# Attention and a gated feed-forward on one core: score matmuls whose weights are widened from 112 to 128 columns

## The chip, the core and the metric

The kernel runs on one core of one Trainium2 chip. The metric is the time of one execution in microseconds on the device. Before the change, the median of six runs is 487.43 us (486.87 to 487.92).

A core has engines that work side by side and meet through semaphores: TensorE (PE) for matmuls, with its weight loads listed on their own (PEld), VectorE (DVE), ScalarE (ACT), GpSimd (POOL) and SyncE (SP). In this kernel POOL issues the loads from memory, and SP issues the transposing DMAs and the stores of the output.

## What is computed

Eight batches of twelve heads, 448 positions of 64 values each. Attention with a squared relu instead of a softmax, then a feed-forward layer with a SiLU gate:

```python
scores = scale * np.matmul(q, k.transpose(0, 1, 3, 2))
attn = np.maximum(scores, 0.0) ** 2 / S
x = np.matmul(attn, v)            # then (batch, seq, heads * dim) = 3584 x 768
xn = x / rms * rms_g
g = xn @ w_gate                   # 768 -> 1536
out = (g * sigmoid(g) * (xn @ w_val)) @ w_out
```

Inputs and output are float32; the kernel's matmuls take bfloat16.

## The kernel before

**Layout.** The two heads of a pair `j` (six pairs) lie one above the other on partitions 0 to 63 and 64 to 127. For each batch a tile `qkT` of shape [128, 6, 2, 448] holds the transposed Q (index 0 of the third axis) and the transposed K (index 1). A position of the sequence is `4 p + c`; the 448 keys are taken as four chunks `c` of 112.

**Scores** (`scores`, line 193) are called for two chunks at a time, so twelve times per batch. For each chunk, two matmuls, one per head, take 112 columns of K as weights and the 448 columns of Q as the moving operand, each with 64 rows: the two heads use the two halves of the array's rows. The profile writes the shape of such weights as 64*112. The results of a chunk fill a PSUM tile `psS` of two banks; two such tiles exist. ScalarE, or VectorE for some last chunks, applies the relu (`r`, lines 211 and 213), and VectorE squares it (line 216).

**The rest of attention.** `attend` (line 224) multiplies the squares with V: weights of 112 rows and 64 columns, two heads side by side on the two halves of the columns. `norm` (line 270) sums squares with a matrix of ones and scales; its result `xn` feeds the feed-forward.

**Feed-forward** (`ffn`, line 340). `gate` and `value` run six matmuls each for each of twelve blocks of 128 columns (`psG`, `psV`, line 295, weights 128*128). `outproj` (line 318) runs twelve matmuls per half tile (`psO`, line 321), ScalarE copies the result, SP stores it.

**Order.** The program's order on each engine is written out by hand. `merge` (line 18) weaves the attention and the norm of batch `b + 1` between the feed-forward units of batch `b`, up to 85% of them. A score call thus stands between gate and value units, or before an `attend`.

**Transposes of Q and K.** Batches 0 and 1 are transposed on TensorE: `transposes` (line 166) writes eight transposes of Q and eight of K for a head pair into one PSUM tile `psT`, and VectorE copies that tile to `qkT`. Batch 1's first step stands at the head of the feed-forward of batch 0. For batches 2 to 7, `transpose_dma` (line 103) issues eight transposing DMAs on SP, four for Q and four for K, after two thirds of the feed-forward of batch `b - 2`. POOL's loads of batch `b + 2` are issued as the feed-forward of batch `b` begins, in the order Q, K, V, into two buffers each.

**Start.** POOL loads Q, K and V of batch 0 in pieces, then the gate and value weights, Q, K and V of batch 1 and the output weights. `keep_busy` puts idle matmuls between the pieces of batch 0.

Of the kernel before, what the change touches and what calls it, by code (L numbers as in the profile page):

```python
# [8 lines left out]
FP32 = mybir.dt.float32  # L9
# [3 lines left out]
ACT = mybir.ActivationFunctionType  # L13
# [23 lines left out]
def kernel(  # L37
# [11 lines left out]
    nc = tc.nc  # L49
    P = nc.NUM_PARTITIONS  # L50
    B, H, S, D = q.shape
# [3 lines left out]
    PC = S // NCH  # L55
# [18 lines left out]
    ps_s = ctx.enter_context(tc.tile_pool(name="ps_s", bufs=2, space=bass.MemoryType.PSUM))  # L74
# [6 lines left out]
    qkT = {}  # L81
# [18 lines left out]
    def new_qkT(b):  # L100
        qkT[b] = qtpool.tile([P, HP, 2, S], BF16, name="qkT", tag="qkT")

    def transpose_dma(b):
        new_qkT(b)
        for ti, nm in enumerate(("q", "k")):
            for c in range(NCH):
                nc.sync.dma_start_transpose(
                    out=qkT[b][:, :, ti, c * PC : (c + 1) * PC], in_=ld[nm, b][:, c, :]
                )
# [56 lines left out]
    def transposes(b, j):  # L166
        if j == 0:
            new_qkT(b)
        psT = ps_m.tile([P, 2, S], BF16, name="psT", tag="mm")
        for ti, nm in enumerate(("q", "k")):  # L170
            for c in range(NCH):
                for hh in range(2):
                    nc.tensor.transpose(  # L173
                        out=psT[hh * D : (hh + 1) * D, ti, c * PC : (c + 1) * PC],
                        in_=ld[nm, b][:, 2 * j + hh, c * D : (c + 1) * D],
                        identity=ident[:],
                    )
        nc.vector.tensor_copy(out=qkT[b][:, j, :, :], in_=psT[:])
# [4 lines left out]
    def relu_on(b, j, c):  # L183
        return "dve" if c == 3 and (b or j % 2) else "act"

    def square_on(b, j, c):
        return "dve"

    def flush():
        while pending:  # L190
            pending.pop(0)()

    def scores(b, j, cs):
        pss = []
        for c in cs:
            psS = ps_s.tile([PC, 2, 512], FP32, name="psS", tag="psS")
            for hh in range(2):
                prt = slice(hh * D, (hh + 1) * D)
                nc.tensor.matmul(  # L199
                    out=psS[:, hh, :S],  # L200
                    lhsT=qkT[b][prt, j, 1, c * PC : (c + 1) * PC],
                    rhs=qkT[b][prt, j, 0, :],
                    start=True,
                    stop=True,
                )
            pss.append(psS)
        squares = []
        for c, psS in zip(cs, pss):
            r = apool.tile([PC, 2, S], BF16, name="r", tag="r")
            if relu_on(b, j, c) == "dve":  # L210
                nc.vector.tensor_relu(out=r[:], in_=psS[:, :, :S])  # L211
            else:
                nc.scalar.activation(out=r[:], in_=psS[:, :, :S], func=ACT.Relu)  # L213
            eng = nc.gpsimd if square_on(b, j, c) == "pool" else nc.vector
            squares.append(
                lambda r=r, eng=eng: eng.tensor_tensor(out=r[:], in0=r[:], in1=r[:], op=ALU.mult)  # L216
            )
            rsq[b, j, c] = r
        flush()
        pending.extend(squares)  # L220
# [25 lines left out]
    def attention(b):  # L246
        units = []

        def add(cost, *fns):
            units.append((cost, lambda: [f() for f in fns]))  # L250

        if b < PE_T:
            add(0.4, lambda: transposes(b, 0))
        for j in range(HP):
            add(0.5, lambda j=j: scores(b, j, (0, 1)))
            if b < PE_T and j + 1 < HP:
                add(0.4, lambda j=j: transposes(b, j + 1))
            if b == 0:
                add(0.3, lambda: keep_busy(2))
            add(1.2, lambda j=j: scores(b, j, (2, 3)), lambda j=j: j and attend(b, j - 1))  # L260
            if b == 0:
                add(0.3, lambda: keep_busy(2))
        add(0.1, flush)
        add(0.8, lambda: attend(b, HP - 1), flush)
        return units
# [88 lines left out]
    for b in range(B):  # L354
        side = []
        if b + 1 < B:
            side = attention(b + 1) + [(1.1, lambda b=b: norm(b + 1))]
        main = ffn(b)
        if b + 2 < B:
            for nm in ("q", "k", "v"):  # L360
                load(nm, b + 2)
            at = len(main) * 2 // 3
            main[at:at] = [(0, lambda b=b: transpose_dma(b + 2))]
        for fn in merge(main, side, 0.0, 0.15):
            fn()
# [30 lines left out]
```

## Time and profile before

| | |
|---|---|
| Median of six runs | 487.43 us |
| The profiled execution, its time | 487.58 us |
| Its span, first to last instruction | 485.8 us |
| Mean granted TensorE clock | 0.986 |
| PE busy | 460.9 us, 95% |
| DVE, ACT, POOL busy | 284.2, 253.6, 50.7 us |
| Score matmuls on the chain that ended last | 9% |

The busy time of an engine is the sum of its instructions' time without overlap. Matmuls are pipelined, so that a busy PE is not PE at its peak. The chain that ended last follows the work back from the last instruction, at each step to what released it or to the instruction before it on its engine. Where a row has three durations, they are the shortest, the middle and the longest in nanoseconds; `x384` counts instructions. A timeline line gives the start and the length of a merged group in microseconds, and in brackets the idle time before it with what ended that. Only what lies within the asked stretch is merged into a line.

### The profile page before, as it was taken

What the parts mean: (1) busy time and instruction counts of PE and PEld (TensorE: products, weight loads), DVE (VectorE), ACT (ScalarE), POOL (GpSimd) and SP (SyncE); (2) the same over time, 40 slices, a digit from 0 to 9 for tenths busy, and PEclk for the clock granted to TensorE, in tenths of its full rate; (3) what the DMA queues carried; (4) which work ended last, traced back from release to release, by engine and by line L of the source; (5) the groups of instructions that cost most, each with busy time, mean ns of one, the idle gap of its engine ahead of it and who ended that gap; (6) DMA issues with size and microseconds to landing.
All of it is one profiled execution on the core that took longest, in us unless ns stands there. A gap on an engine that the chain in (4) does not pass through costs nothing.

```text
span 485.8 us, 7099 instructions
## 1 busy us (share of the span) xinstructions
PE 460.9 (95%) x2872; PEld 220.4 (45%) x2872; DVE 284.2 (59%) x452; ACT 253.6 (52%) x372; POOL 50.7 (10%) x45
## 2 busy tenths in 40 slices
PE   7970999999999999999999999999999999999995
PEld 3420444454445544454445544454445544455553
DVE  2875377756663576765663577765664577662310
ACT  4870355456654566547654566547554566533221
POOL 8323001140001200040001300000000000000000
PEclk9996899999999999999999999999999999999999
DMA  9999999999301990099501992067101300021013
GB/s 108 200 204 199 209 161 135 112 158 178 47 1 36 190 182 9 0 122 198 64 1 34 189 162 33 1 121 119 28 1 34 97 2 0 1 65 34 0 34 97
DMA packets 128032, 43.32 MB, mean 89 GB/s; under 512 B 100608, under 2 KB 124416, under 8 KB 128000
## 3 DMA queue, kind: packets, MB, share of 16 engines
q0 software_dynamic: 88944, 23.60, 50.6%
q1 hardware_dynamic: 39056, 19.28, 21.1%
q8 instruction: 22, 0.36, 0.3%
q14 instruction: 10, 0.08, 0.1%
HBM read 47.19 MB, written 11.01 MB: 120 GB/s over the span
## 4 chain that ended last, share of the span: by engine, by line
PE 87%; DMA 8%; POOL 1%; DVE 1%; ACT 1%; issue 0%; POOLq 0%
PE psG L295 24%; PE psV L295 23%; PE psO L321 22%; PE psS L199 9%; PE psAV L228 8%; DMA kb<-in_k_dram 5%; DMA wv_sb<-in_moe_w_val_dram 3%; PE psSS L273 1%; DVE xn L284 1%; PE psT L173 1%; DVE rstd L281 1%; POOL kb L93 0%; POOL qb L93 0%; ACT r L213 0%; POOL vb L93 0%
## 5 line engine op out<-in xcount | busy, mean ns | idle before, releaser
L213 ACT ACTIVATE r<-psS 112x896 bf16<-112x896 f32 x147 | 128.5, 915 | 47.9 <-PE psS L199 45.0
L295 PE MATMUL psG<-xn,wg_sb 128*128 128x448 bf16 x576 | 127.0, 356 | 0.9 <-DVE xn L284 0.9
L295 PE MATMUL psV<-xn,wv_sb 128*128 128x448 bf16 x576 | 125.7, 355 | 0.0
L312 DVE TENSOR_TENSOR hT<-sil,psV 128x448 bf16<-128x448 bf16 x96 | 59.6, 621 | 99.3 <-PE psV L295 78.3
L321 PE MATMUL psO<-wo_sb,hT 128*128 128x512 bf16 (+1 forms) x672 | 112.9, 326 | 0.0
L216 DVE TENSOR_TENSOR r<-r 112x896 bf16<-112x896 bf16 x192 | 110.0, 618 | 0.2 <-ACT r L213 0.2
L306 ACT ACTIVATE sil<-psG 128x448 bf16<-128x448 f32 x96 | 52.2, 544 | 87.2 <-PE psG L295 86.8
L321 PEld LDWEIGHTS <-hT 128*128 128x128 bf16 x672 | 64.8, 98 | 47.5 <-issue 3.9
L295 PEld LDWEIGHTS <-wv_sb 128*128 128x128 bf16 x576 | 54.2, 98 | 58.1 <-issue 11.2
L295 PEld LDWEIGHTS <-wg_sb 128*128 128x128 bf16 x576 | 51.9, 98 | 62.4 <-issue 18.9
L328 ACT COPY ost<-psO 128x512 f32<-128x512 f32 (+1 forms) x56 | 26.8, 479 | 81.2 <-PE psO L321 81.2
L199 PE MATMUL psS<-qkT 64*112 64x448 bf16 x384 | 57.5, 372 | 3.0 <-ACT r L213 2.3
L211 DVE TENSOR_SCALAR r<-psS 112x896 bf16<-112x896 f32 x45 | 48.9, 1088 | 17.6 <-PE psS L199 17.6
L228 PE MATMUL psAV<-r,vb 112*64 112x448 bf16 x384 | 46.1, 359 | 0.8 <-DVE r L216 0.8
L281 DVE RECIPROCAL rstd<-rstd 128x448 f32<-128x448 f32 x8 | 23.6, 2953 | 22.6 <-ACT rstd L278 22.6
L199 PEld LDWEIGHTS <-qkT 64*112 64x112 bf16 x384 | 18.2, 125 | 38.8 <-issue 35.9
L241 DVE TENSOR_TENSOR x<-xT 128x448 bf16<-128x448 bf16 x48 | 18.6, 386 | 25.1 <-ACT xT L239 25.1
L239 ACT ACTIVATE xT<-psAV 128x448 bf16<-128x448 f32 x48 | 26.1, 544 | 10.4 <-PE psAV L228 7.2
L93 POOL DMA_DIRECT2D vb<-in_v_dram x9 | 8.1, 901 | 212.0 <-PE psAV L228 157.5
L284 DVE SCALAR_TENSOR_TENSOR xn<-xT,g_sb,rstd 128x448 bf16<-128x448 bf16 x48 | 29.3, 680 | 0.3
L228 PEld LDWEIGHTS <-vb 112*64 112x64 bf16 x384 | 17.8, 109 | 24.6 <-issue 16.7
L95 POOL DMA_DIRECT2D qb<-in_q_dram x6 | 13.8, 2304 | 34.8 <-DMA qkT<-kb 32.0
(28 smaller groups left out, 111.2 us busy)
## 6 DMA issues: line engine op xcount, KB each, us to landing
qb<-in_q_dram POOLq DMA_DIRECT2D x7, 672.0 KB, 14.1
kb<-in_k_dram POOLq DMA_DIRECT2D x7, 672.0 KB, 22.5
vb<-in_v_dram POOLq DMA_DIRECT2D x7, 672.0 KB, 9.1
out_dram<-ost SPq DMA_DIRECT2D x8, 336.0 KB, 4.4
wg_sb<-in_moe_w_gate_dram POOLq DMA_DIRECT2D x4, 576.0 KB, 18.5
wv_sb<-in_moe_w_val_dram POOLq DMA_DIRECT2D x4, 576.0 KB, 20.2
wo_sb<-in_moe_w_out_dram POOLq DMA_DIRECT2D x2, 1152.0 KB, 28.7
out_dram<-ost SPq DMA_DIRECT2D x8, 288.0 KB, 4.7
```

Source lines behind the costliest of these rows:

```text
L199: nc.tensor.matmul(out=psS[:, hh, :S], lhsT=qkT[b][prt, j, 1, c * PC : (c + 1) * PC], rhs=qkT[b][prt, j, 0, :], start=True, stop=True,)
L211: nc.vector.tensor_relu(out=r[:], in_=psS[:, :, :S])
L213: nc.scalar.activation(out=r[:], in_=psS[:, :, :S], func=ACT.Relu)
L216: lambda r=r, eng=eng: eng.tensor_tensor(out=r[:], in0=r[:], in1=r[:], op=ALU.mult)
L228: nc.tensor.matmul(out=psAV[hh * D : (hh + 1) * D, :], lhsT=ld["v", b][:, 2 * j + hh, c * D : (c + 1) * D], rhs=rsq[b, j, c][:, hh, :], st ...
L281: nc.vector.reciprocal(out=rstd[:], in_=rstd[:])
L284: nc.vector.scalar_tensor_tensor(out=xn[:, kt, :], in0=xTs[b][:, kt, :], scalar=g_sb[:, kt : kt + 1], in1=rstd[:], op0=ALU.mult, op1=ALU.mult,
L295: nc.tensor.matmul(out=ps[:], lhsT=w_sb[:, kt, fb * P : (fb + 1) * P], rhs=xns[b][:, kt, :], start=(kt == 0), stop=(kt == KT - 1),)
L306: nc.scalar.activation(out=s[:], in_=psG[:], func=ACT.Silu)
L312: nc.vector.tensor_tensor(out=hTs[b // 2][:, fb, o : o + S], in0=sil[b, fb][:], in1=psV[:], op=ALU.mult)
L321: nc.tensor.matmul(out=ps[:, :w], lhsT=hTs[i][:, fk, t * P : (t + 1) * P], rhs=wo_sb[:, fk, o : o + w], start=(fk == 0), stop=(fk == FT - 1),)
L328: nc.scalar.copy(out=ost[:, o : o + w], in_=ps[:, :w])
```

## The change

K now comes first in `qkT` (index 0) and Q second (index 1), on both ways of transposing. The score matmul's weights begin at the chunk's first key, as before, and are 128 columns long: the chunk's 112 keys and the 16 columns that follow in the tile. For the chunks 0 to 2 these are keys of the next chunk, for chunk 3 the first 16 columns of Q. `psS` has 128 partitions, of which the relu reads the first 112. The number of instructions on each engine stays the same.

```diff
 def transpose_dma(b):
-        for ti, nm in enumerate(("q", "k")):
+        for ti, nm in enumerate(("k", "q")):
             for c in range(NCH):
                 nc.sync.dma_start_transpose(
...
 def transposes(b, j):
-        for ti, nm in enumerate(("q", "k")):
+        for ti, nm in enumerate(("k", "q")):
...
 def scores(b, j, cs):
-            psS = ps_s.tile([PC, 2, 512], FP32, name="psS", tag="psS")
+            psS = ps_s.tile([P, 2, 512], FP32, name="psS", tag="psS")
...
-                    lhsT=qkT[b][prt, j, 1, c * PC : (c + 1) * PC],
-                    rhs=qkT[b][prt, j, 0, :],
+                    lhsT=qkT[b][prt, j].rearrange("p t s -> p (t s)")[:, c * PC : c * PC + P],
+                    rhs=qkT[b][prt, j, 1, :],
...
-                nc.vector.tensor_relu(out=r[:], in_=psS[:, :, :S])
+                nc.vector.tensor_relu(out=r[:], in_=psS[:PC, :, :S])
...
-                nc.scalar.activation(out=r[:], in_=psS[:, :, :S], func=ACT.Relu)
+                nc.scalar.activation(out=r[:], in_=psS[:PC, :, :S], func=ACT.Relu)
```

## The prediction

> **What bounds the kernel now.** I read the busy rows of the page first, then the chain that ended last, then the instructions of the score line, and last the timeline of single score calls.
>
> ```profile
> PE 460.9 (95%) x2872; PEld 220.4 (45%) x2872; DVE 284.2 (59%) x452; ACT 253.6 (52%) x372; POOL 50.7 (10%) x45
> ...
> PE 87%; DMA 8%; POOL 1%; DVE 1%; ACT 1%; issue 0%; POOLq 0%
> PE psG L295 24%; PE psV L295 23%; PE psO L321 22%; PE psS L199 9%; PE psAV L228 8%; DMA kb<-in_k_dram 5%; DMA wv_sb<-in_moe_w_val_dram 3%; PE psSS L273 1%; DVE xn L284 1%; PE psT L173 1%; DVE rstd L281 1%; POOL kb L93 0%; POOL qb L93 0%; ACT r L213 0%; POOL vb L93 0%
> ```
>
> TensorE carries 87% of the chain and the score matmuls 9%, so a nanosecond taken from a score call is a nanosecond of the span, except where something else ended last. The 8% of DMA is one stretch at the start: the chain of waits in order of time shows K of batch 1 landing at 48.39 us, eight transposes of it, and then the first gate matmul; from there it is PE nearly without a break. Score calls before 48 us are therefore covered.
>
> What does a score call pay for its weights? The rows of the score line and of the attend line, and the timeline of one call, its successor, and an attend, answer that.
>
> ```profile
> L199 PEld LDWEIGHTS <-qkT x384: 122/123/127, 7.5 to 420.4; 64*112 64x112 bf16 x192
> L199 PE MATMUL psS<-qkT x384: 345/393/394, 7.5 to 420.6; 64*112 64x448 bf16 x192
> ```
>
> ```profile
> L228 PE MATMUL psAV<-r,vb x384: 349/353/378, 13.9 to 427.3; 112*64 112x448 bf16 x192
> ```
>
> ```profile
> 253.21 0.40 PE L199 MATMUL psS<-qkT 64*112 64x448 bf16 x2
> ...
> 253.44 0.35 PE L199 MATMUL psS<-qkT 64*112 64x448 bf16 x2
> 253.73 0.36 PE L295 MATMUL psG<-xn,wg_sb 128*128 128x448 bf16 x1
> ...
> 253.93 0.35 PE L295 MATMUL psG<-xn,wg_sb 128*128 128x448 bf16 x1
> ...
> 256.62 0.38 PE L228 MATMUL psAV<-r,vb 112*64 112x448 bf16 x2
> ...
> 256.83 0.36 PE L228 MATMUL psAV<-r,vb 112*64 112x448 bf16 x2
> ```
>
> A call is two pairs: the two heads run side by side on the two halves of the rows. [...] The open load is the difference between first and second start. Steady 448-column matmuls follow each other every 0.189 us (six psG take 1.31 us). After a change the second starts 0.20 us after the first for 128*128 weights, 0.21 for 64 columns of V, 0.23 for 112 columns of K; to the nanosecond 200, 213 and 233. The durations say the same: the first score pair takes 394 ns against 349 for the second (45 more), the first attend pair 378 against 353 (25 more), the first psG about 10 more. So 64 columns cost 25 ns, 112 columns 45 ns, 0.4 ns a column; full 128 columns cost only 10. The trace also records how a load reads its source: 112 columns as one run, the 128-column loads as four runs of 32. The changed program as built has the four-run form for all 384 score loads.
>
> **The change part by part.**
>
> *The load of 128 columns.* The second pair's load lies under the first pair's matmul in either form, so only one open load counts per call: 8 batches x 6 head pairs x 2 calls = 96 calls, less the 12 of batch 0, which lie before 48 us. Of the 84 left, two lose their gain: around 92 us the second pair of a call waits for ScalarE (the call at 91.55 has its second pair at 92.11, ended by the relu), and ScalarE's order there began with the silu at 89.90, so the call at 89.79 and the first pair at 91.55 give nothing. 82 count. No row shows a 64-row load of 128 columns. Its bounds: the 128*128 row, 10 ns, giving 233 - 200 = 33 ns saved; and 0.4 ns a column, 51 ns, giving 6 ns lost. I take 33, because the form of the load is that of the 128*128 row. 82 x 33 ns = 2.71 us gained.
>
> *Sixteen more columns to drain.* From the second pair to the next kind of matmul it takes 282 ns to psG; from 128*128 psV to a score call also 282, from 64-column psAV to psG 285. No order by columns: between -3 and +4 ns (a 128-column matmul lasts 353, the second score pair 349). I take +2: 82 x 2 = 0.17 us lost.
>
> *K before Q in the PE transposes of batches 0 and 1.* The 16 transposes of a step stand in order on PE, before everything after them. K lands last. Before, Q's eight ran while K was on its way:
>
> ```profile
> 44.96 0.59 PE L173 MATMUL psT<-ident,qb 112*64 112x112 bf16 x8 [10.06 <-DMA qb<-in_q_dram]
> 48.44 0.58 PE L173 MATMUL psT<-ident,kb 112*64 112x112 bf16 x8 [2.89 <-DMA kb<-in_k_dram]
> 48.95 0.93 PE L295 MATMUL psG<-xn,wg_sb 128*128 128x448 bf16 x2
> ```
>
> Now they come after K's. This is on the path: gate matmuls queue behind them. The granted clock there is 0.50 (38.98 to 52.6 us); four pairs of K's transposes start 92 to 97 ns apart, so Q's cost 4 x 93 = 0.37 us. If the clock rises at the same instant as before, the cold work pushed past it runs twice as fast, and 0.19 us is lost; if it rises that much later, 0.37. I take 0.37. The same happens at three waits for K in batch 0, at most 0.37 us each, 1.1 us; that is covered by the wait for K of batch 1: the last xn ends at 42.70 and the first gate matmul starts at 48.95. Without that cover it would be the 1.1 us.
>
> *K before Q in the DMA transposes of batches 2 to 7.* All eight issues of a batch move past each other in SP's queue. For batch 2, SP waited for Q's load until 68.06 and issued K's without waiting at 76.96, so K's landing is between; all eight now start between 68.1 and 77.0, take 14.7 us to issue and at most 10.6 to land: 102.3 at worst, and the first score call of batch 2 is at 107.23. On POOL, the load of Q of batch 3 waits for Q's transposes of batch 2, which now come last: 81.64 becomes at worst 102, its K load a little over 2 us later, V and the loads of batch 4 (98.58 to 101.48) behind them. Landing 22.5 us later and transposed in another 26, batch 3's K and Q stand at 153; its first score call is at 165.60, and SP's next output DMA at 152.28 waits for a late tile anyway. Later batches have their loads landed long before and 30 us between transposes and scores. Cost nothing; without cover it would be the whole delay, up to 20 us once.
>
> *A wider psS, the columns that are not read, the relu on 112 rows.* psS already takes two banks; ScalarE and VectorE read the same 112 rows. The neighbouring columns that a load now also reads (the next keys, or Q behind the last chunk) land with the same batch's transposes. Nothing.
>
> Sum: -2.71 + 0.17 + 0.37 = -2.17 us. The profiled execution took 487.58 us with a span of 485.8; it would become 485.4. It stands 0.15 above the median of the runs, 487.43, which would become 485.3.
>
> [...]
>
> **The rivals.**
>
> *The two halves load one after the other.* Each fast, 2 x 10 ns open: about 23 saved per call, 1.89 - 0.54 = 1.35 us, 486.1 us. For it: no row shows two fast loads at once. Against: the 112-column halves start 2 to 3 ns apart and overlap fully. Chance 0.07.
>
> *Half the rows load at the ordinary rate.* The place is the open first load: 51 ns instead of 45. It costs 82 x 6.4 = 0.53 us, plus 0.54 for drain and start: +1.07, 488.5 us, slower. It decides from the point where the open load takes over about 38 ns (45 less 0.54 us / 82). For it: every load under 128 rows or 128 columns in this trace follows 0.4 ns a column, and none of 64 rows is fast. Against: those loads also had fewer columns and one-run reads. Chance 0.12.
>
> *The clock rises one step later at the start.* From the first gate matmul at 48.95 to the rise at 52.63 the clock stays at 0.50 for 3.7 us. How the rise follows the work is not in the trace; if it came later by that length once more, half of it would be lost, at most 1.8 us, and I price it at 1.7: -2.17 + 1.7, 486.9 us, no change that counts. Against: PE is busy from the same landing of K on. Chance 0.05.
>
> **How the numbers follow.** The forecast has 0.76; its own range is 484.7 to 485.9 (saving 30 to 35 ns, drain -3 to +4 ns, start 0.19 to 0.37 us, and 0.3 us for runs that spread from 486.87 to 487.92). The 8-in-10 range reaches down to 484.5 and up to 486.9, over the serial halves and the late clock, and leaves out the ordinary rate. A measurement of this kernel can tell about 0.2%, 0.97 us, from no change: faster is below 486.46. Forecast and serial halves are faster (0.81 with a little off for the edge), the late clock is no change, and the ordinary rate lies at that edge, mostly slower.
>
> **What would show it.** Right: first score pairs near 360 ns instead of 394, pair starts about 200 ns apart, score loads below 123 ns, and an otherwise equal order of work. The first gate matmul 0.37 us later after K's landing. Wrong: first pairs at 400 ns or more (ordinary rate), near 375 (serial), waits of score loads for a DMA or for the copy of psT, or a clock of 0.50 past 55 us.

## The result: 485.26 us, and the profile after

The changed kernel takes 485.26 us (median of 21 runs) against 487.39 us (44 runs of the kernel before); the ratio is 0.9956, with a 95% interval of 0.9947 to 0.9964. The profiled execution took 486.15 us with a span of 484.4 us.

The page of the changed kernel, its busy row and its chain:

```profile
PE 457.5 (94%) x2872; PEld 213.9 (44%) x2872; DVE 284.1 (59%) x452; ACT 253.2 (52%) x372; POOL 50.7 (10%) x45
...
PE 86%; DMA 8%; POOL 1%; DVE 1%; ACT 1%; issue 0%; POOLq 0%
PE psG L296 24%; PE psV L296 23%; PE psO L322 22%; PE psS L200 8%; PE psAV L229 8%; DMA kb<-in_k_dram 5%; DMA wv_sb<-in_moe_w_val_dram 3%; PE psSS L274 1%; DVE xn L285 1%; PE psT L173 1%; DVE rstd L282 1%; POOL kb L93 0%; POOL qb L93 0%; ACT r L214 0%; POOL vb L93 0%
```

The instruction counts of the busy row are the same, and of the chain's lines only the score line gave something up (9% to 8%). PE is busy 3.4 us less, more than the time fell, since this sum also counts the twelve calls of batch 0, which lie under waits. Where in a call that happened is read from the score line's own rows (shortest, middle, longest duration):

```profile
L200 PEld LDWEIGHTS <-qkT x384: 91/93/97, 7.9 to 418.9; 64*128 64x128 bf16 x192
L200 PE MATMUL psS<-qkT x384: 345/359/361, 7.9 to 419.1; 64*128 64x448 bf16 x192
```

A load takes 93 ns instead of 123. The longest matmul, that of a first pair, which carries the open load, went from 394 ns to 361. The timeline shows one call: last psV, first pair, second pair, attend.

```profile
255.49 0.35 PE L296 MATMUL psV<-xn,wv_sb 128*128 128x448 bf16 x1
255.77 0.36 PE L200 MATMUL psS<-qkT 64*128 64x448 bf16 x2
...
255.97 0.35 PE L200 MATMUL psS<-qkT 64*128 64x448 bf16 x2
256.25 0.38 PE L229 MATMUL psAV<-r,vb 112*64 112x448 bf16 x2
```

The pairs start 0.20 us apart instead of 0.23. Over the 84 calls of batches 1 to 7 the middle values in the trace's nanoseconds are:

| ns, middle of 84 calls | before | after |
|---|---|---|
| previous matmul to first pair | 282 | 285 |
| first pair to second pair | 233 | 200 |
| second pair to the next kind | 284 | 284 |

So a call gives back 33 ns and takes 3. In the changed kernel each half's first matmul starts 4 ns after its own load; before, it was 1 to 2 ns. The two halves' loads start 3 ns apart in both kernels, so that now both precede the first matmul. The second pair's loads start 189 ns ahead of their matmuls (187 before), under the first pair's.

At the start, the transposes of batch 1 and the first gate matmuls of the changed kernel:

```profile
49.35 0.58 PE L173 MATMUL psT<-ident,kb 112*64 112x112 bf16 x8 [14.33 <-DMA kb<-in_k_dram]
49.72 0.58 PE L173 MATMUL psT<-ident,qb 112*64 112x112 bf16 x8
50.24 1.30 PE L296 MATMUL psG<-xn,wg_sb 128*128 128x448 bf16 x3
```

Q's eight transposes now stand between K's and the gate: 0.89 us from K's first transpose to the first gate matmul, against 0.51 before. K itself landed 0.9 us later in this execution; a second profile of the same kernel had it at 48.62, close to the 48.44 of the kernel before.

The queues of SP and POOL after the new order, from the timeline:

```profile
74.43 6.48 SPq L107 DMA_TRANSPOSE qkT<-kb  x4
80.96 5.26 SPq L107 DMA_TRANSPOSE qkT<-qb  x4
```

```profile
88.52 2.28 POOL L95 DMA_DIRECT2D qb<-in_q_dram  x1 [37.97 <-DMA qkT<-qb]
```

SP now waits for K's load and starts at 74.43 instead of 68.14; Q of batch 3 is loaded from 88.52 instead of 81.64. Neither is late: batch 2's first score call runs at 107.96 and waits for nothing there.

### The profile page after: what moved, and what is told of

Read it like the earlier page. It is cut to its first block, busy times and chain, and to the rows that moved or that the text cites. A ratio compares the mean times of both kernels' runs of the same rounds, so it can differ in the third digit from the quotient of the medians.

```text
span 484.4 us, 7098 instructions
## 1 busy us (share of the span) xinstructions
PE 457.5 (94%) x2872; PEld 213.9 (44%) x2872; DVE 284.1 (59%) x452; ACT 253.2 (52%) x372; POOL 50.7 (10%) x45
## 4 chain that ended last, share of the span: by engine, by line
PE 86%; DMA 8%; POOL 1%; DVE 1%; ACT 1%; issue 0%; POOLq 0%
PE psG L296 24%; PE psV L296 23%; PE psO L322 22%; PE psS L200 8%; PE psAV L229 8%; DMA kb<-in_k_dram 5%; DMA wv_sb<-in_moe_w_val_dram 3%; PE psSS L274 1%; DVE xn L285 1%; PE psT L173 1%; DVE rstd L282 1%; POOL kb L93 0%; POOL qb L93 0%; ACT r L214 0%; POOL vb L93 0%
## 5 line engine op out<-in xcount | busy, mean ns | idle before, releaser
L214 ACT ACTIVATE r<-psS 112x896 bf16<-112x896 f32 x147 | 128.3, 914 | 46.4 <-PE psS L200 46.1
L212 DVE TENSOR_SCALAR r<-psS 112x896 bf16<-112x896 f32 x45 | 48.9, 1088 | 16.7 <-PE psS L200 16.7
L200 PE MATMUL psS<-qkT 64*128 64x448 bf16 x384 | 54.2, 355 | 3.5 <-ACT r L214 2.8
L200 PEld LDWEIGHTS <-qkT 64*128 64x128 bf16 x384 | 11.7, 94 | 39.6 <-issue 37.7
L173 PE MATMUL psT<-ident,kb 112*64 112x112 bf16 x96 | 4.8, 226 | 15.3 <-DMA kb<-in_k_dram 15.3
```

Of the source, the lines that this page charges most:

```text
L200: nc.tensor.matmul(out=psS[:, hh, :S], lhsT=qkT[b][prt, j].rearrange("p t s -> p (t s)")[:, c * PC : c * PC + P], rhs=qkT[b][prt, j, 1, :] ...
L212: nc.vector.tensor_relu(out=r[:], in_=psS[:PC, :, :S])
L214: nc.scalar.activation(out=r[:], in_=psS[:PC, :, :S], func=ACT.Relu)
```

## Experiments

The theory: all of the gain is the open weight load of a score call, fast at 128 columns but not at 112 or 127, and the K-first order of the transposes costs 0.37 us at the start. The rivals: the gain comes of the order, of a wide psS, or of every load; and the fast load suffers from half rows or odd places.

Total times alone cannot part these by 0.1%, since runs of one kernel spread by 1 to 3.5 us. So I also took from each profile the stretch between the first gate matmuls of neighbouring batches, which holds twelve score calls and no part of the start. Three such stretches, and the time from the first pair to the second:

| kernel | pair to pair, ns | batch 2 to 3, us | 3 to 4 | 6 to 7 |
|---|---|---|---|---|
| before | 233 | 52.91 | 56.81 | 52.30 |
| after, two profiles | 200 | 52.54 | 56.44 | 51.96 |
| order only, 112 columns | 233 | 52.91 | 56.81 | 52.30 |
| Q transposed first, two profiles | 200 | 52.54 | 56.44 | 51.96 |
| 127 columns | 241 | 53.00 | 56.90 | 52.38 |
| 128 columns for one head | 200 and 234 | 52.91 | 56.81 | 52.30 |
| 128 columns in the first pair | 200 | 52.54 | 56.44 | 51.96 |
| 128 columns in the second pair | 233 | 52.91 | 56.81 | 52.30 |
| chunks of a call swapped | 200 | 52.54 | 56.44 | 51.96 |

The stretches repeat to 0.01 us between executions. The second distance of the kernel with one wide head is that of its narrow head, counted from the call's first matmul. 0.34 to 0.37 us for twelve calls is 28 to 31 ns a call, the 30 of the table before.

**Order only.** K first in tile and transposes, 112 columns.

```diff
-psS = ps_s.tile([P, 2, 512], ...)
+psS = ps_s.tile([PC, 2, 512], ...)
-lhsT=qkT[b][prt, j].rearrange("p t s -> p (t s)")[:, c * PC : c * PC + P],
+lhsT=qkT[b][prt, j, 0, c * PC : (c + 1) * PC],
```

> Both orders (tile and transposes) are K first, the weights stay 112 columns. Theory (the gain is the open weight load of a call): no gain is left, second pairs start 233 ns after first ones as before, and the start pays 0.37 us: 487.8 us, 0.1% over the kernel before, hardly to be told from it. The profile shows the first gate matmul about 0.89 us after K of batch 1 has landed, against 0.51 before. Rival (the gain comes of where K and Q stand, not of the load): 485.3 us.

Measured: 488.29 us against 487.85 on the same chip, ratio 1.0009 (0.9995 to 1.0024). Each stretch is that of the kernel before, and from K's first transpose to the gate it takes 0.89 us. The order gives nothing; the rival falls.

**Q transposed first**, K still first in the tile; run twice, the second time beside the changed kernel itself.

```diff
-for ti, nm in enumerate(("k", "q")):
+for ti, nm in ((1, "q"), (0, "k")):
```

> As the changed kernel, but Q is transposed first again on both ways; K still stands first in the tile. Theory: keeps the loads (pair starts 200 ns apart) and gets back the 0.37 us of Q's transposes at half clock after K has landed: 484.9 us, and the first gate matmul 0.51 us after K's landing. Rival (the lost time at the start is only a later landing of K, which has nothing to do with the order): 485.3 us.

> The changed kernel itself, on the same chip as the next three, so that they can be set beside it. 0.4% to 0.5% under the kernel before; between the first score call's two pairs 200 ns, first gate matmul 0.89 us after K's landing.

> Q transposed first again, beside the changed kernel on one chip. Theory: 0.37 us less at most (0.08%), of which half comes back where the clock rises at the same instant: 0.1 to 0.4 us under the changed kernel. Runs spread by 1 to 3 us, so the time may not tell; the profile must, with 0.52 us from K's landing to the first gate matmul, not 0.89.

The first time 485.61 us against 487.85 for the kernel before, ratio 0.9949 (0.9932 to 0.9965). On the second chip 485.30 us, 0.9961 (0.9949 to 0.9974), beside 485.34 us, 0.9965 (0.9953 to 0.9978), of the changed kernel, which is a little less than the 0.4% to 0.5% expected of it. By time the two kernels cannot be told apart, and both medians with Q first lie nearer to the rival's 485.3 than to 484.9. The profile of the first run tells:

```profile
44.63 0.59 PE L173 MATMUL psT<-ident,qb 112*64 112x112 bf16 x8 [10.18 <-DMA qb<-in_q_dram]
48.11 0.59 PE L173 MATMUL psT<-ident,kb 112*64 112x112 bf16 x8 [2.89 <-DMA kb<-in_k_dram]
48.63 0.93 PE L296 MATMUL psG<-xn,wg_sb 128*128 128x448 bf16 x2
```

0.52 us from K to the gate in both runs, against 0.89 in both profiles of the changed kernel, so the gate's delay of 0.37 us is real and comes of the order. In these profiles the clock outweighs it: with Q first it rose 5.5 us after the first gate matmul both times, in the two of the changed kernel after 3.2 and 2.9. If I take the time from K's first transpose to the end and subtract half of the half-clock time after the first gate matmul, 435.54 us remain before, 435.88 with the order only, 433.41 and 433.40 after, and 432.94 twice with Q first. So, counted at an equal clock after the gate, the order costs 0.34 to 0.47 us, and the loads bring 2.48 to 2.60.

How much of the 0.37 us reaches the end is another question. In the eleven profiles without the warm start below, the half clock that ends there lasted 10.24, 13.65 or 17.07 us (once, seven and three times), three, four or five times 3.41 us, a third of the shortest. In these profiles the rise thus came in whole steps from the drop, and a gate that comes 0.37 us later need not move it. The gate work that the delay pushes past the rise would then run at 1.00 instead of 0.50 (in the changed kernel the steady gate and value matmuls start 373 ns apart before the rise and 189 behind it), half of the 0.37 would be made good, and an estimated 0.19 us would be lost. The runs are too few and too far apart to show which it is.

**127 columns.**

```diff
-out=psS[:, hh, :S],
+out=psS[: P - 1, hh, :S],
-... [:, c * PC : c * PC + P],
+... [:, c * PC : c * PC + P - 1],
```

> 127 columns instead of 128. Theory (a load is fast at 128 columns alone; otherwise it costs 0.4 ns a column): open load 51 ns, second pairs start 239 ns after first ones, score loads of 127 ns or more; 82 calls lose 6 ns and the start 0.37 us: 488.3 us. Rival (a wide load is fast by its width, or a wide psS is what helps): pair starts about 200 ns apart and 485.3 us.

```profile
L200 PEld LDWEIGHTS <-qkT x384: 130/130/134, 8.4 to 420.0; 64*127 64x127 bf16 x192
L200 PE MATMUL psS<-qkT x384: 346/401/401, 8.4 to 420.2; 64*127 64x448 bf16 x192
```

488.23 us against 487.85, ratio 1.0006 (0.9994 to 1.0019). One column fewer than 128, and a load takes 130 ns instead of 93, the first pair 401 instead of 361: 52 ns of open load over the 349 of a covered matmul, at 0.41 ns a column. Each stretch is 0.08 to 0.09 us longer than before. So neither width nor the wide psS makes a load fast. Of the widths tried (64, 112, 127 and 128, with 25, 45, 52 and 11 ns open) only 128 is fast; but at 128 the load also reads its source as four runs of 32, at 127 as one run, and no kernel here has the one without the other. With the half clock taken off as above 436.54 us remain, 0.66 more than with the order only, which is 82 times the 8 ns.

**128 columns for one head of a pair.**

```diff
+w = P if hh == 0 else PC
-out=psS[:, hh, :S],
+out=psS[:w, hh, :S],
-... [:, c * PC : c * PC + P],
+... [:, c * PC : c * PC + w],
```

> 128 columns for the first head of a pair, 112 for the second. Theory (the two halves of the rows load side by side, a pair is ready when its slower half is): the second pair starts 233 ns after the first for the second head, nothing is gained: 487.7 us. Rival (the halves share one path, loads add up): half of the gain, pair starts near 216 ns, 486.6 us.

488.95 us, ratio 1.0022 (1.0009 to 1.0036). The timeline of one call, asked so that first the second matmul of the wide head and then that of the narrow one begins the line:

```profile
255.09 0.39 PE L201 MATMUL psS<-qkT 64*128 64x448 bf16 x2
...
255.29 0.38 PE L201 MATMUL psS<-qkT 64*128 64x448 bf16 x2
...
255.32 0.35 PE L201 MATMUL psS<-qkT 64*112 64x448 bf16 x1
255.60 0.36 PE L297 MATMUL psG<-xn,wg_sb 128*128 128x448 bf16 x1
```

Each half goes at its own pace: the wide head's second matmul at 200 ns, the narrow head's at 234, and the next kind waits for the later one. The loads of the two halves do not add up, which would have put the pairs near 216 ns apart and given half of the gain; the stretches are those of the kernel before. The total lies 1.25 us above what was expected. After K's landing nothing of that is seen: with the half clock taken off 435.92 us remain, as with the order only (435.88). In the one execution that was profiled K landed late (first transpose at 50.04); for the other runs there is no trace.

**128 columns in the first or in the second pair only.**

```diff
+w = P if c == cs[0] else PC      # the other kernel: cs[1]
-out=psS[:, hh, :S],
+out=psS[:w, hh, :S],
-... [:, c * PC : c * PC + P],
+... [:, c * PC : c * PC + w],
```

> Only the first chunk of a call has 128 columns, the second has 112. Theory (only the open load counts, the second pair's load lies under the first pair's matmul): all of the gain stays: pair starts 200 ns apart, 485.3 us and stretches between the batches' first gate matmuls as in the changed kernel (52.54 and 56.44 us). Rival (each of the loads counts): half of the gain, 486.3 us and 52.72 and 56.62 us.

> Only the second chunk of a call has 128 columns, the first has 112. Theory (the second pair's load is hidden anyway): no gain at all: pair starts 233 ns apart, stretches between the batches' first gate matmuls of 58.37, 52.91 and 56.81 us as in the kernel before, and 487.8 us with the 0.37 us at the start. Rival (each load counts): 486.6 us.

First pair only: 485.58 us, ratio 0.9962 (0.9947 to 0.9976), everything kept. Second pair only: 488.59 us, 1.0017 (0.9998 to 1.0036), nothing gained. With the half clock taken off, 433.41 and 435.90 us remain. Their matmul rows, the first kernel's and the second's:

```profile
L201 PE MATMUL psS<-qkT x384: 346/359/393, 7.6 to 418.6; 64*128 64x448 bf16 x96, 64*112 64x448 bf16 x96
```

```profile
L201 PE MATMUL psS<-qkT x384: 346/360/394, 8.4 to 420.0; 64*112 64x448 bf16 x96, 64*128 64x448 bf16 x96
```

The rows look alike, with the same mix of forms: the three durations of a row do not tell which pair paid. The distances between starts do, 200 against 233.

**Chunks of a call swapped**, so that the open load begins at column 112 or 336.

```diff
-scores(b, j, (0, 1))
+scores(b, j, (1, 0))
-scores(b, j, (2, 3))
+scores(b, j, (3, 2))
```

> Each call takes its chunks in the other order, so that the open load begins at column 112 or 336 of a row (224 or 672 bytes, no multiple of 64) and not at 0 or 224 columns (0 or 448 bytes). The relu on VectorE then comes first in a call. Theory (a fast load's time does not depend on where it begins): pair starts 200 ns apart, 485.3 us give or take 0.3 for the other order of the relus. Rival (a fast load that begins at an odd place is slower): pair starts up to 233 ns apart and up to 487.8 us.

485.79 us, ratio 0.9972 (0.9959 to 0.9985); pairs 200 ns apart, all stretches as after. Where a load begins does not matter for the places tried: 200 ns from columns 112 and 336 as from 0 and 224. The total is 0.2 us above the range that was expected. The clock in its profile rose 5.2 us after the first gate matmul; with that taken off as above, 433.36 us remain, the changed kernel's value to 0.05 us.

**A warm start.** The clock is what is left at the start, so the last kernel keeps PE running while it waits for batch 1, with Q transposed first.

```diff
-merge([], attention(0) + [(1.1, lambda: norm(0))])
+merge([], attention(0) + [(1.1, lambda: norm(0)), (0, lambda: keep_busy(62))])
```

> As the kernel with Q transposed first, and 62 idle matmuls (11.7 us at 189 ns) between the norm of batch 0 and the wait for Q and K of batch 1, so that PE does not idle from 34.9 to 48 us. Theory (what is left at the start is the half clock after that idle time, which lasts 2.7 to 5.5 us past the first gate matmul, so that K's landing and the clock make the runs differ): clock 1.00 at the first gate matmul, eight transposes and the change of kind in about 0.36 us instead of 0.52, 1.3 to 2.8 us gained: about 483.2 us, 0.9% under the kernel before. Rival (the clock drops anyhow, or the idle matmuls end after K's landing): 485.3 us or more.

482.89 us against 487.73, ratio 0.9903 (0.9884 to 0.9923): the fastest of all, though of four runs only. Its timeline, and its windows (length, busy time and count of PE, PEld, DVE, ACT, POOL, then the granted clock, DMA share and GB/s); after them a window of the changed kernel that also lies behind its first gate matmul:

```profile
34.59 11.89 PE L139 MATMUL psB<-busy_bf,ones_bf 128*128 128x448 bf16 x62
46.41 0.39 PE L173 MATMUL psT<-ident,qb 112*64 112x112 bf16 x8
48.47 0.39 PE L173 MATMUL psT<-ident,kb 112*64 112x112 bf16 x8 [1.67 <-DMA kb<-in_k_dram]
48.79 1.31 PE L296 MATMUL psG<-xn,wg_sb 128*128 128x448 bf16 x6
```

```profile
48.90:52.60 3.70, 3.70 (x21) 1.60 (x20) 1.25 (x2) 1.57 (x3) 0.77 (x1) 1.00 1.27 209
```

```profile
50.30:53.40 3.10, 3.10 (x11) 1.27 (x10) 0.62 (x1) 0.54 (x1) 0.25 (x1) 0.50 1.18 211
```

The idle matmuls end before K lands, the clock stands at 1.00 when the gates begin (six take 1.31 us, where the changed kernel's timeline has 2.42), and K to gate takes 0.32 us.

## Why the prediction was right, step by step

- **PE carries the end.** Right. What a call lost on PE came off the stretches between batches, 28 to 31 ns a call, and the two calls before 92 us gained nothing up to the relu: the second pair of the call at 91.55 still waits for it (586 ns after the first instead of 557). One thing was left out: that pair's own load lies open after the wait, and the attend behind it comes 296 ns later instead of 327. These 31 ns, once, are within the rounding.
- **The open load, 33 ns a call.** Right to the nanosecond, 233 to 200. The choice between the two bounds rested on the four-run form of the load; the 127-column kernel, which reads in one run, paid 52 ns where the other bound had 51 for 128. That half rows go fast, two halves at once, was not in the trace before; the changed kernel shows it, with loads of 93 ns that start 3 ns apart. In both kernels' traces, for score, attend, gate and value matmuls, the first load after a change of the weights' shape starts 2 to 4 ns ahead of its matmul and the later loads 187 to 189 ns ahead, under the matmul before (middle values); so one load of a call lies open.
- **Only one load a call counts.** Right, shown by the first-pair and second-pair kernels, 200 and 233 ns.
- **Drain, 2 ns a call.** The size was near by luck, the cause was wrong. No run shows that PE drains at a change, or that more columns prolong it: with the wider weights nothing changed behind a call (284 and 284). The traces show 282 to 288 ns from start to start where score, attend and gate or value matmuls follow each other, and 189 from gate to value, whose weights have one shape. The 3 ns lie ahead of the call and go with a fast load in the first pair: 285 there, but 282 with 127 columns or with 128 in the second pair only. 82 x 3 is 0.25 us against the 0.17 of the sum.
- **Q's transposes after K's landing, 0.37 us.** The delay is right: 0.89 against 0.51 us, shown both by the order alone and by turning it back. That all of it reaches the end is not shown; by the steps in which the clock rose, the 0.19 that the prediction also named is as likely. The three waits in batch 0 stayed covered: the last xn of batch 0 began at 42.14 us instead of 42.02, long before K's landing.
- **DMA order, nothing.** Right: with the order only, each stretch is that of the kernel before. SP's first transposes at 74.43 lie within the 68.1 to 77.0 that was given.
- **The sum.** -2.71 + 0.25 + 0.37 = -2.09 us with the measured terms, against -2.17; with 0.19 for the start it is -2.27. The medians differ by 2.13, and by the interval of the ratio anything from 1.8 to 2.6 is possible. The size is confirmed, the agreement to a few hundredths is luck.
- **The rivals.** Halves one after the other: no, 200 ns. Ordinary rate: no, but 127 columns, with 241 ns, are what it would have looked like. The clock rising later was not seen in the two profiles of the changed kernel. It rises anywhere from 2.0 to 5.5 us after the first gate matmul in the eleven profiles without the warm start, the kernel before at 3.7. That rival was a term of noise in every kernel, and I had listed it as a case.

At the full clock 128 columns left 11 ns of a load open and 127 left 52; 112 and 127 columns showed 0.40 and 0.41 ns a column. At the half clock the difference was larger: the call at 12.41 us of the kernel with the order only has its pairs 415 ns apart, the one at 12.38 us of the swapped kernel, with 128 columns, 347, so that 112 columns cost 68 ns more there than 128, not 33. In the kernel before the first two gate matmuls at a clock of 0.50, with 128 columns, start 346 ns apart.

## What to carry to other kernels

Look at the first load after each change of kind of matmul: the distance from the first to the second matmul, less the steady distance, is what lies open, and only that can be gained. Here it was 233 less 189 ns, and 33 of these 44 were gained. If the weights have nearly 128 columns and neighbouring data that may be read, try the full 128, and see in the trace whether the load reads in four runs of 32, as the fast ones did here. 127 columns did not do (241 ns against 200), and the loads under a running matmul needed no change (233 ns with only the second pair wide, as before). Before reordering inputs that arrive one after the other, ask which lands last: work on the early one belongs ahead of that wait. Behind it, at a granted clock of 0.50, Q's eight transposes put the first gate matmul 0.37 us later; on a warm clock of 1.00 eight transposes took 0.39 us from first to last instead of 0.58.

## What I had not expected

- The two halves of the rows are independent down to the load: with 128 columns in one half and 112 in the other, the second matmuls start 200 and 234 ns after the first.
- The start makes the spread of the runs. In the eleven profiles without the warm start, K's first transpose of batch 1 came between 47.53 and 50.04 us, and the half clock lasted 2.0 to 5.5 us past the first gate matmul. At half speed the latter alone is 1.7 us of difference, nearly the size of the change. Over the executions of the changed kernel the sixteen with a mean granted clock of 0.984 or 0.985 average 485.06 us, the six with 0.982 average 486.07; the mean does not say where the half clock lay. Filling the idle stretch from 34.6 to 46.4 us with matmuls took the clock's part away: in the warm start's profile it stood at 1.00 from 34.9 to 48.4 us and from 48.9 to 52.6.
